# Duo attention with a maxout FFN: masks ahead of the scores, the flags on another queue, and batch 0 rearranged

## The chip, the cores and the metric

The kernel runs on one core of a Trainium2 chip. The metric is the time of one execution in device microseconds (us), as the median of several runs. A profile is taken of one execution; its times count from the start of the span, which is some 2 us shorter than the time of the run. Engines: PE is TensorE's matmuls, PEld its weight loads, DVE is VectorE, ACT is ScalarE, POOL is GpSimd, SP is SyncE. "ACTq", "SPq" and "POOLq" are the queues on which these engines issue transfers.

## The reference

Four batches of eight heads, 768 positions of 64 numbers. Each head is either a "retrieval" head (causal mask) or a "streaming" head (causal, and only the first 4 keys or the last 64 count). Which kind a head is comes as an input, `is_retrieval`, eight integers; below they are called the **flags**. The attention output of all tokens goes through a maxout FFN.

```python
scores = q @ k.T / sqrt(64)
mask   = causal if is_retrieval[h] else causal & (is_sink | in_window)
a      = softmax(where(mask, scores, -1e9))
x      = (a @ v)                      # (4, 8, 768, 64) -> 3072 tokens x 512
h      = maximum(maximum(x @ w1, x @ w2), x @ w3)      # 512 -> 768
out    = h @ w_out                                     # 768 -> 512
```

## The kernel before

The kernel works through 16 score tiles t = 0 to 15: batch, then half of the queries, then four heads. In each it computes transposed scores on PE, exponentiates on ACT, masks on POOL, multiplies by V on PE (with a column of ones that gives the row sums), and divides on DVE. The FFN of a half batch, 18 units of four matmuls and then 3 output blocks, is kept in a queue, and `fill(n)` puts n units of it between the attention work so that PE has something to do while it waits. "FFN (0,0)" below is the FFN of the first half of batch 0, "FFN (0,1)" that of its second half. Instructions are issued to every engine in the order of the program.

The start loads the flags first, on ACT's queue, then K and Q of the four head pairs of batch 0, then V. The weights, the second half of batch 0 and K and Q of the later batches go through POOL's "software" queue, which casts to fp16 where the target is fp16; V of the later batches stays on SP's queue:

```python
nc.scalar.dma_start(out=ir32, in_=is_retrieval ... .to_broadcast([P, 2 * H]))   # the flags
load_pairs(0, 0, 1, (nc.sync, nc.scalar))      # half, first pair, pairs, (queue of K, queue of Q)
load_pairs(0, 1, 1, (nc.sync, nc.scalar))
load_pairs(0, 2, 2, (nc.sync, nc.scalar))
load_v(0, 0)
# ...
def head_flags():                              # first thing that DVE does with data
    nc.vector.tensor_scalar(out=RT, in0=ir32[:, 0 : 2 * H : 2], scalar1=0.0, ..., op0=ALU.not_equal)
    # ... least, far
def head_masks(hp, early=False):               # the two masks of a head pair, from the flags
    # ... nc.vector.tensor_scalar(out=mk[:, h], in0=kept, scalar1=least[:, h : h + 1], ...)
```

K and Q of batch 0 are cast (`cast_pair`), transposed on PE into one PSUM bank, and copied out together (`turn_pair`). For the first two tiles (`NQ` is 2; they are slots 0 to 3) the mask is added in PSUM by an identity matmul that stands after the scores:

```python
def scores(t, u, pairs=(0, 1)):
    early = t < NQ
    # ... the score matmuls:
        nc.tensor.matmul(sts[g // m][...], KQ[rows, 0, ...], KQ[rows, 1, ...],
                         start=(c0 == 0 and r == 0), stop=((b == 0 or r == 1) and not early), ...)
    # ...
        if early:
            # ... nc.tensor.matmul(st[...], ident, mk[...], start=False, stop=True, ...)
        nc.scalar.activation(out=pts[t, i][...], in_=st[...], func=AF.Exp, scale=sc)
```

The order of the start, and the order in the loop over "slots" (one slot is one exp group; slots 4 to 11 belong to batch 0, slot 12 is the first of batch 1):

```python
head_flags()
cast_pair(0, 0, (dve, act))
for hp in range(2):
    head_masks(hp, True)
turn_pair(0, 0, dve)
cast_pair(0, 1, (pool, act))
turn_pair(0, 1, dve)
scores(0, 0, (0,))
cast_pair(0, 2, (dve, pool))
cast_pair(0, 3, (pool, pool))
load_weight(0)                                  # w0t: POOL issues it after its casts
# ... scores, AV, more loads; FFN (0,0) is queued by the last turn_x(1, 1)
fill(2)
for hp in range(2):
    turn_pair(1, hp, dve)
fill(2)
# the loop:
    put(o + (8 if late else 6) + i, late, prep_v, 4 * b + 2, i)      # V casts, on DVE
    put(o + 10 + i, 2, prep_v, 4 * b + 3, i)
    # batch 1's K and Q come in fp16 and are transposed by DVE (eight times 1.14 us):
    put(o + (10 if b == 0 else 8) + 2 * qd + x, 1, turn, b + 1, qd, x, p)
def pace(n):                                    # FFN units per slot
    return 2.4 if n < 14 else 4.0
```

The softmax here doesn't subtract the row's maximum and nothing guards it: scores larger than these inputs give would overflow.

## Time and profile before

| | before |
|---|---|
| time, median of 3 runs | 213.36 us (213.06 to 213.45) |
| span of the profiled run | 211.6 us |
| PE busy | 197.5 us, 93% |
| matmuls | 2132 |

The page's share of the granted TensorE clock in 40 slices (each 5.3 us, in tenths), and its list of what the chain that ended last consists of:

```profile
PEclk9999999999699999999999999999999999999999
PE 74%; DMA 8%; DVE 8%; ACT 4%; issue 2%; POOL 1%; ACTq 0%; DVEq 0%
```

The 6 in the eleventh slice is the spell at half clock that the prediction below speaks of, from 54.3 to 57.7 us in the trace's clock records; it is the only one that this row shows. (The row has no record of the first 6.5 us, where 12 idle matmuls of 512 columns take 5.30 us, twice the 216 ns each that such a matmul takes later.) Lines of the timeline: start, duration, engine and line, what it writes and reads, and in brackets how long the engine had been idle and what ended that.

```profile
0.80 0.42 ACTq L207 DMA_DIRECT2D ir<-in_is_retrieval_dram  x1
...
4.56 0.17 DVE L266 TENSOR_SCALAR RT<-ir 128x8 f32<-128x8 int32 x1 [1.23 <-DMA ir<-in_is_retrieval_dram]
...
...
6.35 0.41 PE L149 MATMUL tr<-ident,kn 128*128 128x128 f16 x3
```

The flags are issued first (0.80), land at 4.54, and DVE makes RT from them at once. K and Q of the first pair land at 5.05 and about 5.8, and PE's first real work, the transposes, starts at 6.35.

### The profile page before, as it was taken

Reading aid. Unit: us, or ns where it says so; the run is one execution under the profiler, and the core shown is the slowest. Engines: PE = TensorE matmul, PEld = TensorE weight load, DVE = VectorE, ACT = ScalarE, POOL = GpSimd, SP = SyncE. Lnnn points to the kernel's source line nnn. Section 1 sums busy time; section 2 is a strip of 40 time slices with the busy share of each in tenths; the row PEclk is TensorE's granted clock in tenths of the full one; section 3 lists DMA queues with packets and bytes.
Section 4 is the critical chain, followed back from the end, with each engine's and each line's share of the span. In section 5 each row is a group of like instructions: output and inputs, shape, how many; then the busy total and the mean of one; then the engine's idle time right before and its main releaser. Section 6 shows DMA issues by size and latency. Waiting matters only on the chain.

```text
span 211.6 us, 5225 instructions
## 1 busy us (share of the span) xinstructions
PE 197.5 (93%) x2132; PEld 112.6 (53%) x2132; DVE 136.5 (65%) x287; ACT 120.5 (57%) x178; POOL 130.0 (61%) x156
## 2 busy tenths in 40 slices
PE   7896889976799999999999999999999999999992
PEld 2454444635456546556566455565565466565550
DVE  3867758689577607996595609996576336554640
ACT  2480896665436686565556675664756766622222
POOL 3399469859994872559995844479944914820000
PEclk9999999999699999999999999999999999999999
DMA  3979999997029568201249397002100120012003
GB/s 103 311 120 277 279 269 213 210 244 219 5 34 164 102 167 230 56 0 54 99 77 156 67 279 173 0 0 102 51 3 0 54 99 3 0 49 103 0 0 150
DMA packets 32396, 23.93 MB, mean 113 GB/s; under 512 B 22837, under 2 KB 27253, under 8 KB 32373
## 3 DMA queue, kind: packets, MB, share of 16 engines
q0 software_dynamic: 4784, 10.23, 24.2%
q1 hardware_dynamic: 26372, 12.59, 20.8%
q10 hardware_dynamic: 1216, 0.79, 1.3%
q8 instruction: 16, 0.26, 0.5%
q14 instruction: 8, 0.06, 0.1%
HBM read 25.17 MB, written 6.29 MB: 149 GB/s over the span
## 4 chain that ended last, share of the span: by engine, by line
PE 74%; DMA 8%; DVE 8%; ACT 4%; issue 2%; POOL 1%; ACTq 0%; DVEq 0%
PE yy L326 37%; PE yy L344 12%; PE st L410 10%; PE oacc L471 8%; DVE KQ L183 4%; PE tr L497 3%; DMA qs<-in_q_dram 3%; ACT pt L432 3%; DMA vs<-in_v_dram 3%; PE yst L326 3%; DMA ks<-in_k_dram 2%; PE yst L344 1%; DVE acc L337 1%; DVE x L481 1%; ACT acc L334 1%
## 5 line engine op out<-in xcount | busy, mean ns | idle before, releaser
L455 POOL TENSOR_TENSOR pt<-pt,mk 128x512 f16<-128x512 f16 x84 | 90.6, 1104 | 35.3 <-ACT pt L432 32.2
L432 ACT ACTIVATE pt<-st 128x1024 f16<-128x1024 f32 (+3 forms) x98 | 83.2, 904 | 23.9 <-PE st L410 20.7
L337 DVE TENSOR_TENSOR acc<-yy,acc 128x384 f16<-128x384 f32 x45 | 25.0, 557 | 39.7 <-ACT acc L334 29.6
L326 PE MATMUL yy<-xT,w0t 128*128 128x384 f16 x180 | 37.1, 331 | 0.3 <-DMA w0t<-in_moe_w_dram 0.3
L334 ACT CAST acc<-yy 128x384 f16<-128x384 f32 x45 | 21.5, 483 | 27.6 <-PE yy L326 23.2
L326 PE MATMUL yy<-xT,w1t 128*128 128x384 f16 x180 | 36.8, 329 | 0.0
L326 PE MATMUL yy<-xT,w2t 128*128 128x384 f16 x180 | 36.3, 326 | 0.0
L410 PE MATMUL st<-KQ 32*128 32x384 f16 (+5 forms) x560 | 29.3, 282 | 5.0 <-DVE rc L479 1.5
L344 PE MATMUL yy<-woutt,hT 128*128 128x512 f16 x132 | 31.6, 379 | 0.0
L337 DVE TENSOR_TENSOR hT<-yy,acc 128x384 f16<-128x384 f32 x45 | 25.0, 557 | 4.3 <-PE yy L326 2.0
L471 PEld LDWEIGHTS <-pt 128*128 128x128 f16 x672 | 24.8, 97 | 5.1 <-issue 1.3
L410 PEld LDWEIGHTS <-KQ 32*128 32x128 f16 (+1 forms) x560 | 12.3, 93 | 24.5 <-issue 15.1
L183 DVE STREAM_TRANSPOSE KQ<-kq 128x384 f32<-128x384 f32 x24 | 24.8, 1138 | 0.0
L471 PE MATMUL oacc<-va,pt 128*128 128x65 f16 x352 | 24.8, 193 | 0.0
L351 ACT COPY ot<-yy 128x512 f32<-128x512 f32 x22 | 13.0, 589 | 20.2 <-PE yy L344 17.4
L326 PEld LDWEIGHTS <-w1t 128*128 128x128 f16 x192 | 17.9, 99 | 12.0 <-issue 2.0
L326 PEld LDWEIGHTS <-w0t 128*128 128x128 f16 x192 | 17.6, 99 | 11.9 <-issue 1.7
L326 PEld LDWEIGHTS <-w2t 128*128 128x128 f16 x192 | 17.6, 98 | 10.4 <-issue 0.4
L471 PE MATMUL oacc<-vf,pt 128*128 128x65 f16 x320 | 21.2, 193 | 0.7 <-DVE hT L337 0.7
L344 PEld LDWEIGHTS <-hT 128*128 128x128 f16 x144 | 13.2, 98 | 14.9 <-issue 1.0
L376 POOL TENSOR_TENSOR vf<-va,far 128x384 f16<-128x384 f16 x16 | 13.2, 826 | 11.8 <-DVE va L374 11.8
L481 DVE TENSOR_TENSOR x<-oacc,rc 128x384 f16<-128x384 f32 x32 | 17.8, 557 | 1.1
(60 smaller groups left out, 139.3 us busy)
## 6 DMA issues: line engine op xcount, KB each, us to landing
out_dram<-ot SPq DMA_DIRECT2D x24, 256.0 KB, 2.2
vs<-in_v_dram SPq DMA_DIRECT2D x21, 256.0 KB, 5.1
kq<-in_k_dram POOLq DMA_DIRECT2D x6, 384.0 KB, 6.3
kq<-in_q_dram POOLq DMA_DIRECT2D x6, 384.0 KB, 7.6
w0t<-in_moe_w_dram POOLq DMA_DIRECT2D x1, 768.0 KB, 8.2
ks<-in_k_dram POOLq DMA_DIRECT2D x2, 384.0 KB, 7.6
qs<-in_q_dram POOLq DMA_DIRECT2D x2, 384.0 KB, 7.8
w1t<-in_moe_w_dram POOLq DMA_DIRECT2D x1, 768.0 KB, 8.7
```

The source lines that it names most:

```text
L183: nc.vector.transpose(out=dst.rearrange("c (p j) -> c j p", j=n)[:, j0:j1], in_=src.rearrange("c (j i) -> c j i", i=R),)
L326: nc.tensor.matmul(yy[:, 0:HALF], w_t[wi][:, ks, ni * P : (ni + 1) * P], xT[b, half][ks], start=(ks == 0), stop=(ks == KS - 1),)
L334: nc.scalar.copy(out=acc[ni], in_=yy[:, 0:HALF])
L337: nc.vector.tensor_tensor(out=dst, in0=yy[:, 0:HALF], in1=acc[ni], op=ALU.max)
L344: nc.tensor.matmul(yo[:, 0:DMdl], hT[ns][:, tb * P : (tb + 1) * P], woutt[:, ns, :], start=(ns == 0), stop=(ns == NNB - 1),)
L351: nc.scalar.copy(out=ot, in_=yo[:, 0:DMdl])
L376: nc.gpsimd.tensor_tensor(out=vf[j][:, hs, k0:k1, 0:D], in0=vs[:, hs, 0:1] if half == 0 else va[j][:, hs, k0:k1, 0:D], in1=far[:, hs, k0:k ...
L410: nc.tensor.matmul(sts[g // m][:, g % m, c0 : c0 + n * P], KQ[rows, 0, ki * P : (ki + 1) * P], KQ[rows, 1, t0 : t0 + n * P], start=(c0 == ...
L432: nc.scalar.activation(out=pts[t, i][:, u, h0 : h0 + m, 0:w], in_=st[:, :, 0:w], func=AF.Exp, scale=sc,)
L455: nc.gpsimd.tensor_tensor(out=x, in0=x, in1=m, op=ALU.mult)
L471: nc.tensor.matmul(o[:, qi, hl, 0 : D + 1], pt[:, u, hl, c : c + P], vv[:, 2 * hp + hl, ki, 0 : D + 1], start=(idx == 0), stop=(idx == len ...
L481: nc.vector.tensor_tensor(out=x, in0=o[:, :, :, 0:D], in1=rc.unsqueeze(3).to_broadcast([P, HB, 2, D]), op=ALU.mult,)
```

## The change

Its intent is to shorten the first 58 us, where PE isn't always busy. (1) The masks enter PSUM first, and the scores are added to them, so that the exp can follow the scores directly. (2) K and Q of the first pair are copied out of PSUM separately. (3) The flags are loaded through GpSimd, so that Q can be issued first on ACT's queue; K and Q of pairs 2 and 3 come in two transfers each. (4) The first tiles' scores, casts and x copies are reordered, some moved to ACT. (5) In the loop of batch 0, V casts go from DVE to ACT, DVE's transposes for batch 1 start earlier, and the FFN units are spread differently.

```diff
-    def load_pairs(half, hp, n, engines):
+    def load_pairs(half, hp, n, engines, alone=False):
+            m = 2 if alone else 2 * n          # (cut: one transfer per pair if alone)
-    def turn_pair(half, hp, op, parts=((0, 1),)):
+    def turn_pair(half, hp, *engines):         # (cut: one bank and one copy per engine given)
-    nc.scalar.dma_start(
+    nc.gpsimd.dma_start(
         out=ir32,
-    load_pairs(0, 2, 2, (nc.sync, nc.scalar))
+    load_pairs(0, 2, 2, (nc.sync, nc.scalar), True)
     # in scores():
+        for x, st in sts.items() if early else ():
+            first = True
+            # (cut) ... ident, mk[...], start=first, stop=False
-                        start=(c0 == 0 and r == 0),
-                        stop=((b == 0 or r == 1) and not early),
+                        start=(c0 == 0 and r == 0 and not early),
+                        stop=(b == 0 or r == 1),
-            if early:
-                # (cut) ... ident, mk[...], start=False, stop=True
     # the start (cut to a part of it):
-    for hp in range(2):
-        head_masks(hp, True)
-    turn_pair(0, 0, dve)
+    head_masks(0, True)
+    turn_pair(0, 0, dve, dve)
-    cast_pair(0, 2, (dve, pool))
+    cast_pair(0, 2, (act, pool))
     for i in range(2):
         prep_v(0, i, pool)
-    load_pairs(1, 0, 2, (nc.gpsimd, nc.gpsimd))
-    # (cut) scores and AV, which move too
     for i in range(2):
         prep_v(1, i, dve)                      # has a multiplication on POOL each
+    load_pairs(1, 0, 2, (nc.gpsimd, nc.gpsimd))
     # (cut)
-    turn_x(0, 0)
-    turn_x(0, 1)
+    turn_x(0, 0, act)
+    turn_x(0, 1, act)
-    fill(2)
+    fill(4)
     # the loop:
-                put(o + i, 2, prep_v, 2 * NQ * b, i)
+                put(o + i, 2, prep_v, 2 * NQ * b, i, act if b == 1 else None)
-            put(o + 10 + i, 2, prep_v, 4 * b + 3, i)
+            put(o + 10 + i, 2, prep_v, 4 * b + 3, i, act if b == 0 else None)
     # (cut: two more lines of the same kind)
-                        put(o + (10 if b == 0 else 8) + 2 * qd + x, 1, turn, b + 1, qd, x, p)
+                        if b == 0:
+                            n, place = 10 + 2 * qd + x, "x" if qd else (0, "x")[p] if x == 0 else 0
+                        else:
+                            n, place = o + 8 + 2 * qd + x, 1
+                        put(n, place, turn, b + 1, qd, x, p)
-        return 2.4 if n < 14 else 4.0
+        return 2.4 if n < 8 else 1.6 if n < 11 else 3.0 if n < 14 else 3.6 if n < 20 else 4.0
```

More of the change, by code (lines that the diff above doesn't have):

```diff
@@ L114 @@
     KQs = {}
-    def load_pairs(half, hp, n, engines):
+    def load_pairs(half, hp, n, engines, alone=False):
         for nm, src, eng in zip(("ks", "qs"), (k, q), engines):
             st = stage.tile([P, 4, HB, D], FP32, tag=nm, name=nm)
-            eng.dma_start(
-                out=st[:, 0 : 2 * n],
-                in_=src[
-                    0, 2 * hp : 2 * hp + 2 * n, half * HALF : (half + 1) * HALF
-                ].rearrange("h (p j) d -> p h j d", p=P),
-            )
+            m = 2 if alone else 2 * n
+            for h in range(0, 2 * n, m):
+                eng.dma_start(
+                    out=st[:, h : h + m],
+                    in_=src[
+                        0, 2 * hp + h : 2 * hp + h + m, half * HALF : (half + 1) * HALF
+                    ].rearrange("h (p j) d -> p h j d", p=P),
+                )
             for i in range(n):
@@ L138, in of_pair @@
         ].rearrange("p (i t) -> p i t", i=2)
-    def turn_pair(half, hp, op, parts=((0, 1),)):
+    def turn_pair(half, hp, *engines):
         if (0, hp // 2) not in KQs:
             KQs[0, hp // 2] = qkt.tile([P, 2, S, 2], FP16, tag="KQ", name="KQ")
-        tr = bank([P, 1024], FP16, "tr")
         xs = cast.pop((half, hp))
-        for part in parts:
-            for i in part:
+        n = 2 // len(engines)
+        for part, op in enumerate(engines):
+            tr = bank([P, 1024], FP16, "tr")
+            for i in range(n):
                 for j in range(HB):
@@ L149, in turn_pair @@
                     nc.tensor.transpose(
-                        tr[:, c : c + P], xs[i][:, j].rearrange("p h d -> p (h d)"), ident
+                        tr[:, c : c + P],
+                        xs[part + i][:, j].rearrange("p h d -> p (h d)"),
+                        ident,
                     )
-            i0, i1 = part[0], part[-1] + 1
             op(
-                out=of_pair(hp)[:, i0:i1, half * HALF : (half + 1) * HALF].rearrange(
-                    "p i (t j) -> p i t j", j=HB
-                ),
-                in_=tr[:, i0 * HALF : i1 * HALF].rearrange(
-                    "p (i j t) -> p i t j", i=i1 - i0, j=HB
-                ),
+                out=of_pair(hp)[
+                    :, part : part + n, half * HALF : (half + 1) * HALF
+                ].rearrange("p i (t j) -> p i t j", j=HB),
+                in_=tr[:, 0 : n * HALF].rearrange("p (i j t) -> p i t j", i=n, j=HB),
             )
@@ L393, in scores @@
                 pts[t, i] = ptp.tile([P, 4, 2, 512], FP16, tag="pt", name="pt")
-        m = 1 if t == 0 and u == 1 else 2
+        m = 1 if u == 1 and (t == 0 or t == 1 and pairs == (0,)) else 2
         if m == 1:
@@ L400, in scores @@
             sts = {i: sps.tile([P, 2, 512], FP32, tag="st", name="st") for i in pairs}
+        for x, st in sts.items() if early else ():
+            first = True
+            for _, u0, _, cols, n, m0 in MASKED[0]:
+                if u0 != u:
+                    continue
+                for hl in range(m):
+                    nc.tensor.matmul(
+                        st[:, hl, cols[0] : cols[0] + n],
+                        ident,
+                        mk[:, 4 * qd + m * x + hl, m0 : m0 + n],
+                        start=first, stop=False, skip_group_check=True,
+                    )
+                first = False
         todo = [(i, part) for i in (pairs if b == 0 else (0,)) for part in UNITS[half][u]]
@@ L420, in scores @@
             i, h0 = m * x // 2, m * x % 2
-            if early:
-                for _, u0, _, cols, n, m0 in MASKED[0]:
-                    if u0 != u:
-                        continue
-                    for hl in range(m):
-                        nc.tensor.matmul(
-                            st[:, hl, cols[0] : cols[0] + n],
-                            ident,
-                            mk[:, 4 * qd + m * x + hl, m0 : m0 + n],
-                            start=False, stop=True, skip_group_check=True,
-                        )
             nc.scalar.activation(
@@ L485, in av, with turn_x @@
         xs[t, i] = x
-    def turn_x(t, i):
+    def turn_x(t, i, op=None):
         b, half, qd = where(t)
@@ L499, in turn_x @@
             )
-        nc.vector.tensor_copy(out=xT[b, half][hp], in_=tr[:, 0:HALF])
+        (op or nc.vector.tensor_copy)(out=xT[b, half][hp], in_=tr[:, 0:HALF])
         if hp == NHP - 1:
@@ L512 @@
     head_flags()
+    head_masks(0, True)
     cast_pair(0, 0, (dve, act))
-    for hp in range(2):
-        head_masks(hp, True)
-    turn_pair(0, 0, dve)
+    head_masks(1, True)
+    turn_pair(0, 0, dve, dve)
     cast_pair(0, 1, (pool, act))
     turn_pair(0, 1, dve)
+    cast_pair(0, 2, (act, pool))
     scores(0, 0, (0,))
-    cast_pair(0, 2, (dve, pool))
+    turn_pair(0, 2, dve)
+    scores(0, 0, (1,))
+    head_masks(2, True)
+    scores(0, 1, (0,))
     cast_pair(0, 3, (pool, pool))
     load_weight(0)
-    head_masks(2, True)
-    scores(0, 0, (1,))
-    turn_pair(0, 2, dve)
-    scores(0, 1, (0,))
     turn_pair(0, 3, dve)
     head_masks(3, True)
+    scores(0, 1, (1,))
     scores(1, 0, (0,))
-    scores(0, 1, (1,))
     scores(1, 0, (1,))
+    scores(1, 1, (0,))
     for i in range(2):
         prep_v(0, i, pool)
-    load_pairs(1, 0, 2, (nc.gpsimd, nc.gpsimd))
-    scores(1, 1, (0,))
-    av(0, 0)
-    av(0, 1)
-    scores(1, 1, (1,))
     for i in range(2):
         prep_v(1, i, dve)
+    load_pairs(1, 0, 2, (nc.gpsimd, nc.gpsimd))
+    av(0, 0)
+    scores(1, 1, (1,))
+    av(0, 1)
     load_weight(1)
     load_pairs(1, 2, 2, (nc.gpsimd, nc.gpsimd))
-    turn_x(0, 0)
-    turn_x(0, 1)
     av(1, 0)
+    turn_x(0, 0, act)
+    turn_x(0, 1, act)
     av(1, 1)
@@ L558 @@
         head_masks(hp)
-    fill(2)
+    fill(1)
     FIRST = 4
@@ L571 @@
             if b > 0:
-                put(o + i, 2, prep_v, 2 * NQ * b, i)
-                put(o + 2 + i, 2, prep_v, 2 * NQ * b + 1, i)
+                put(o + i, 2, prep_v, 2 * NQ * b, i, act if b == 1 else None)
+                put(o + 2 + i, 2, prep_v, 2 * NQ * b + 1, i, act if b == 1 else None)
                 put(o + i, 1, av, 4 * b - 1, i)
@@ L580 @@
             late = 1 if b == 0 else 0
-            put(o + (8 if late else 6) + i, late, prep_v, 4 * b + 2, i)
-            put(o + 10 + i, 2, prep_v, 4 * b + 3, i)
+            put(o + (8 if late else 6) + i, late, prep_v, 4 * b + 2, i, act if b == 0 else None)
+            put(o + 10 + i, 2, prep_v, 4 * b + 3, i, act if b == 0 else None)
             put(o + 8 + late + i, 1, av, 4 * b + 2, i)
```

## The prediction

> **What bounds the kernel now.** I read the page first (busy shares, then the chain that ended last), then the engines' busy times by stretch, then the timeline of the first 60 us, and last the landings of the transfers. The page has PE busy 93% of 211.6 us and 74% of the chain. The stretches show where the other part lies (us; then busy time and count of PE, weight loads, DVE, ACT, POOL; granted clock, DMA share, GB/s):
>
> ```profile
> 8.00:16.00 8.00, 7.44 (x90) 4.40 (x87) 5.97 (x12) 5.97 (x10) 6.37 (x12) 1.00 0.89 172
> 16.00:19.40 3.40, 1.91 (x34) 1.35 (x35) 3.16 (x11) 0.31 (x1) 3.40 (x6) 1.00 1.11 318
> 19.40:43.00 23.60, 22.00 (x217) 12.23 (x217) 15.79 (x34) 17.53 (x25) 17.71 (x20) 1.00 1.12 240
> 43.00:49.00 6.00, 4.06 (x40) 1.72 (x37) 5.81 (x10) 2.68 (x4) 3.59 (x4) 1.00 1.05 253
> 49.00:55.40 6.40, 4.20 (x94) 3.15 (x91) 6.19 (x11) 3.15 (x5) 6.40 (x9) 0.91 0.40 124
> 55.40:58.00 2.60, 2.60 (x16) 1.32 (x14) 0.60 (x2) 2.18 (x3) 2.60 (x4) 0.56 0.01 3
> 130.20:203.90 73.70, 73.66 (x794) 43.39 (x794) 46.02 (x95) 38.75 (x60) 37.74 (x40) 1.00 0.10 37
> ```
>
> From 58 to 204 us PE has work always. Before that it hasn't: from 43 to 55.4 us it is busy 8.3 of 12.4 us while DVE is busy 12.0, and right after it runs at 0.56 of its clock. Busy time hides part of it, so I also took the distance between the starts of neighbouring matmuls, less what each streams (162 ns for 384 columns, 216 for 512, 56 for 128, 32 for an AV matmul, 95 more at a switch between full-height and short tiles). Lost that way: 2.3 us on the half-clock idle matmuls of the start, 5.9 us between 6.5 and 25, 1.3 between 25 and 45, 5.3 between 45 and 58, about 2.5 in all the rest, of which two times 0.5 at 83 and 129 us. A part that touches the first 58 us has some 12 us to win at the very most; PE's own work (about 190 us) is unchanged. The timeline names the waits:
>
> ```profile
> 17.42 0.56 DVE L481 TENSOR_TENSOR x<-oacc,rc 128x384 f16<-128x384 f32 x1
> ...
> 18.03 0.34 PE L497 MATMUL tr<-ident,x 128*128 128x128 f16 x3 [0.58 <-DVE x L481]
> ...
> 19.36 1.47 PE L326 MATMUL yy<-xT,w0t 128*128 128x384 f16 x8 [0.29 <-DMA w0t<-in_moe_w_dram]
> ...
> 21.86 0.34 PE L149 MATMUL tr<-ident,qn 128*128 128x128 f16 x3 [0.58 <-ACT qn L132]
> ...
> 48.42 0.63 PE L410 MATMUL st<-KQ 32*128 32x384 f16 x16 [1.49 <-DVE KQ L183]
> ...
> 54.19 1.00 PE L410 MATMUL st<-KQ 32*128 32x384 f16 x16 [1.51 <-DVE rc L479]
> ```
>
> The last two are the scores of batch 1, which need eight DVE transposes (1.14 us each, from 43.86 to 54.1); the one put down to rc really waits for the transposes just ahead of it, which end at 54.1. No FFN work stands between, as all of FFN (0,0) was issued by 46.5 us. The chain shows the price of the lull:
>
> ```profile
> 55.62 2.39 PE yy L326 x8
> 58.01 0.37 PE oacc L471 x12
> 58.38 1.30 PE yy L326 x8
> ```
>
> Eight FFN matmuls take 2.39 us here and 1.30 anywhere later.
>
> **What the Trainium skill says.** "TensorE: Matmul & The Clock Gate", Part 1, says that an idle window of about 3.4 us drops the array to half clock. The trace agrees in kind: a 3.4 us spell at half clock begins at 54.3 us, though PE was not wholly idle before it. "PSUM — Partial Sum Buffer", The four PSUM rules, says that the first matmul's flag clears a whole bank's marks and later matmuls overwrite unmarked columns and add to marked ones; so the mask may come first and costs what it cost when last. No run shows it yet. "DMA: Bandwidth & Descriptors", Issuing engines are not separate DMA queues, says that another issuer saves sequencer time alone. The trace agrees: the flags' issue took 0.42 us on ACT and Q's first issue came at 1.25 us. "Perfetto Trace Analysis", Optimizing Scalar/DVE Operations, allows moving work to ScalarE where DVE is saturated; here DVE was busy 5.81 of 6.00 us.
>
> **The change part by part.** The order of the built programs gives the same 2132 matmuls; only places and engines move.
>
> *Masks first.* 24 identity matmuls move ahead of the scores. They ran after them in 0.50 us per head pair of 1024 columns. For the first pair I expect nearly nothing: in the new order they stand behind the transposes of pair 1, which end at about 8.0 us because of the Q cast at 7.22, so mask and score still follow each other and the first exp comes at about 8.9 us (8.93 now). The same holds for K and Q evacuated apart (0.96 us becomes two of about 0.5): KQ came at 7.92, pair 1's transposes at 7.95. 0 to 0.3 us.
>
> *Flags by GpSimd, K/Q of pairs 2 and 3 in two transfers each.* Q issues 0.42 us earlier, but landings are spaced by bandwidth (5.05, 6.66, 7.20, 8.37, 9.51 us), so pair 2 may land 0.6 to 1 us earlier and pair 3 as before. POOL's last cast then ends at about 10.0 instead of 11.12 us, where the w0t load is issued. Between 10.6 and 15.9 us the DMA moves only 120 GB/s, from then on some 250 without pause until 45 us: a weight load issued 1 us earlier moves this whole queue (w0t 19.31, ks 20.23, qs 21.21, kq of batch 1 40.29 and 44.33) up to 1 us forward.
>
> *Exp chain and x copies.* ACT's exps of t=0,1 run from 8.93 to 16.31 with 1.0 us idle; without gaps after the second they end at about 15.9. Two of four xT copies (0.35 us) go to ACT and DVE's V casts go ahead of the reciprocals, so DVE's tail from the last exp to the last xT shortens from 3.15 to about 2.8 us. The first FFN matmul starts at about 18.7 instead of 19.36: 0.65 us.
>
> *Four FFN units instead of two before the K/Q transposes.* PE lost 0.27 and 0.74 us there, waiting for ks and qs. Two more units of 0.65 us cover it: 1.2 us. Start to 25 us: 0.65 + 1.2 = about 1.9 us.
>
> *V casts on ACT, transposes earlier, FFN slower.* Eight casts of 0.4 to 0.6 us leave DVE between 36 and 60 us (ACT's Q cast of the same shape took 0.53). The first DVE transpose now stands before slot 10 and no longer behind slot 11's x. Batch 1's first scores (slot 12) have three limits. ACT: from slot 4's exps on, 16 exps (12 of 1.03, 4 of 0.76), one acc copy, 2 Q casts, 2 output copies and 4 V casts of 0.45 sum to 19.9 us, from 23.4 to 24.4: 43.3 to 44.3. DVE: kq's Q half lands at 39.3 to 40.3, then x of 0.75 and two transposes: 43.5 to 44.7. PE: about 42.6. So slot 12 comes at about 44 instead of 48.42, with one FFN unit group of 1.29 us still undone: ahead by 3.1 us. From there: scores 0.65, that group 1.29, AV 0.95, slot 13; slot 14 waits for the last two transposes at about 49.4 to 50, and FFN (0,1) starts at 51 to 52 instead of 55.41. That is 3.4 to 4.4 us, with the gain of the start (1.9) inside. If the lulls, now about 1 us each, no longer trip the half clock, 1.3 us more (eight times 0.16).
>
> After that PE is saturated and the FFN pace only shifts work: 0 (perhaps 0.3 either way at 83 us). Sum: 3.9 (middle) + 0.8 x 1.3 (chance of no half clock) + 0.1 = 5.0 us. 213.36 - 5.0 = **208.3 us**.
>
> **The rivals.** (a) *ACT takes the place of DVE.* It gets eight V casts and two xT copies, and was busy 17.53 of 23.6 us in the main stretch; if exps slip behind casts that wait for V, slots 8 to 12 wait for ACT. For it: 0.7 and 0.5 us of exp-related lulls are already there. Against: ACT is busy 8.0 of the 15 us from 43 to 58. It would leave slot 12 at about 46 and the time at 210 to 210.5. (b) *The DMA sets slot 12 and 14.* If kq lands no earlier, DVE waits at the head of the transposes, its order then holding hT and xT up, and the lull only moves. For it: DMA share above 1.0 from 16 to 45 us. Gain then about 3 us and the half clock may stay: 210.3. (c) *Everything falls in.* Exps start at 8.4, no half clock, the 0.5 us at 83 goes too: 7 us, 206.3. (d) *No gain*, as later work takes it back: PE is full from 58 us on with no wait on another engine, so what is won before must show at the end; unlikely.
>
> **Range and chances.** (a) and (b) together I give 35%, the main line 50%, (c) 15%. Two per cent is 4.2 us, so below about 209.2 counts as faster: main line and (c), with some overlap each way. Time 208.3, range 206.2 to 211.0; faster 0.66, same 0.32, slower 0.02.
>
> **What would show it.** Right: in the chain, the first FFN matmul at 18.4 to 19.0; no wait of PE for the Q cast near 21 us; w0t issued near 10 us; DVE's eight transposes from about 38 to 50 us; the first 16-matmul scores of batch 1 at 43.5 to 45; FFN (0,1) at 51 to 52; eight FFN matmuls there in 1.30, clock 1.00 throughout; the end of the trace after 200 us like before. Wrong: PE's waits of 1 us or more at slots 12 and 14 named ACT or DMA; a half-clock spell after 7 us; w0t landing at 19.3 as before; a first exp at 8.5 or earlier (I undersized the mask part); a new lull after 60 us from the slower FFN pace.

## The result, and the profile after

The changed kernel took 210.86 us (median of 4 runs, 210.43 to 211.60), the kernel before 213.21 us in the runs that go with it. Executions over 1.5% slower than the fastest of the same kernel are left out of the means. Throughout this document a ratio is the mean time of one kernel's runs over that of the other's runs of the same rounds, so it isn't quite the ratio of the medians quoted. Here it is 0.9895, with a 95% interval of 0.9861 to 0.9929: a gain of 2.35 us by the medians, where 5.0 had been forecast. All outputs were correct, here and in every experiment below.

The page's clock row and chain of the changed kernel:

```profile
PEclk9979999999999999999999999999999999999998
PE 80%; DVE 10%; DMA 3%; ACT 2%; issue 1%; POOL 1%; POOLq 0%; ACTq 0%
PE yy L328 38%; PE yy L346 13%; PE st L425 10%; PE oacc L475 9%; DVE KQ L185 5%; PE tr L501 3%; DMA ir<-in_is_retrieval_dram 3%; PE yst L328 3%; DVE x L485 2%; ACT pt L436 2%; PE tr L152 2%; PE st L409 1%; PE yst L346 1%; DVE KQ L157 1%; DVE rc L483 1%
```

The half-clock slice at 55 us is gone, as hoped. A new one stands third from the left: the clock records have half clock from 9.9 to 13.3 us, right after PE stood idle from 6.56 to 9.81. And a name has come into the chain that wasn't listed before: the transfer of the flags, with 3% of the span, for 8 KB. The timeline of the start:

```profile
1.32 0.72 POOL L209 DMA_DIRECT2D ir<-in_is_retrieval_dram  x1 [0.81 <-POOLq L649]
...
8.11 0.17 DVE L268 TENSOR_SCALAR RT<-ir 128x8 f32<-128x8 int32 x1 [3.54 <-DMA ir<-in_is_retrieval_dram]
...
9.81 0.46 PE L152 MATMUL tr<-ident,kn 128*128 128x128 f16 x3 [3.25 <-POOL kn L134]
```

Q is issued 0.44 us earlier, as predicted, and the first K and Q land at 4.02 and 4.25 instead of 5.05 and about 5.8. But the flags, issued at 1.32, land at 8.09: 6.8 us from issue to landing, where ACT's queue had needed 3.7. RT is DVE's first instruction that needs data. DVE works in order, so its cast of K waits behind it (and behind the first pair's masks, which the change put ahead of the cast) although K is there, and the first transposes start at 9.81 instead of 6.35. (The bracket names POOL's cast, which ended at nearly the same moment; the weight load ahead of it waited for DVE's kn.)

That isn't all. One stretch of the kernel before (us; busy time and count of PE, weight loads, DVE, ACT, POOL; granted clock, DMA share, GB/s):

```profile
5.00:6.00 1.00, 1.00 (x4) 0.38 (x3) 0.95 (x5) 0.17 (x1) 0.47 (x2) 1.00 1.01 330
```

And three of the changed one:

```profile
4.00:5.00 1.00, 1.00 (x3) 0.29 (x2) 0.34 (x3) 0.78 (x3) 0.00 (x0) 1.00 1.06 213
5.00:6.00 1.00, 1.00 (x4) 0.29 (x2) 0.00 (x0) 0.00 (x0) 0.00 (x0) 1.00 0.95 64
6.00:7.00 1.00, 0.56 (x2) 0.00 (x0) 0.00 (x0) 0.00 (x0) 0.00 (x0) 1.00 0.65 143
```

The last number of a line is the rate at which data moved. It falls to 64 GB/s, where the kernel before had 330, while the DMA engines are still "busy" 95% of the time. In the queues' view of the first 12 us of the changed kernel one sees with what (packets, MB, share of 16 engines):

```profile
q1 hardware_dynamic: 4023, 1.53, 49.7%
...
q0 software_dynamic: 32, 0.01, 9.4%
```

32 packets with a hundredth of a megabyte took 9.4% of the engines' time, 18 us in all (0.094 x 12 x 16), where the 1.53 MB on SP's queue, K and V, took 49.7%. The 16 that carry data (512 bytes each) took 0.38 to 1.77 us, 1.1 on average. So the transfer of the flags through GpSimd was late itself, and while it ran little else moved. The second Q landed at 8.27 instead of 7.20, and all four pairs were there at 10.26 instead of 9.51.

The middle of the batch went much as forecast. The stretches that the prediction shows, now:

```profile
8.00:16.00 8.00, 5.89 (x51) 3.92 (x52) 6.92 (x17) 3.70 (x7) 6.19 (x14) 0.79 0.97 192
...
43.00:49.00 6.00, 5.80 (x69) 2.97 (x68) 5.97 (x11) 4.45 (x9) 4.75 (x6) 1.00 0.93 218
49.00:55.40 6.40, 4.89 (x99) 3.41 (x98) 4.70 (x9) 4.78 (x8) 6.40 (x8) 1.00 1.06 272
55.40:58.00 2.60, 2.60 (x27) 1.60 (x25) 1.10 (x4) 1.63 (x3) 2.60 (x4) 1.00 0.67 149
```

From 43 to 55.4 us PE is busy 10.7 us instead of 8.3, and the clock is 1.00 from 49 to 58 us. From 8 to 16 us, on the other hand, PE is busy 5.89 us instead of 7.44, at a clock of 0.79. The points along the way, in us:

| | before | after |
|---|---|---|
| first transpose of K | 6.35 | 9.81 |
| first FFN matmul, FFN (0,0) | 19.36 | 22.05 |
| first scores of batch 1, slot 12 | 48.42 | 47.84 |
| first matmul of FFN (0,1) | 55.41 | 55.04 |

The changed kernel is 2.7 us behind at its first FFN matmul and 0.6 ahead at slot 12. By the measure of the prediction (the distance between the starts of neighbouring matmuls, less what each streams) PE loses 9.75 us before 25 us where it lost 8.3, 1.8 from 25 to 45 where it lost 1.3, and 2.2 from 45 to 60 where it lost 5.3. With the rest of the span that is 15.8 instead of 17.6 us, and the difference, 1.8, fits that of the two spans (211.6 - 209.9 = 1.7). So from 25 us on 2.6 us were won, of the 3.1 that the prediction's sum gives to the loop and the clock, and the start, meant to win 1.9, lost about 1.5.

### The profile page after: what moved, and what is told of

It is laid out like the page before. It is cut to its first block, busy times and chain, and to the rows that moved or that the text cites. A ratio compares the mean times of both kernels' runs of the same rounds, so it can differ in the third digit from the quotient of the medians.

```text
span 209.9 us, 5236 instructions
## 1 busy us (share of the span) xinstructions
PE 196.0 (93%) x2132; PEld 112.7 (54%) x2132; DVE 132.1 (63%) x277; ACT 125.1 (60%) x190; POOL 129.4 (62%) x157
## 3 DMA queue, kind: packets, MB, share of 16 engines
HBM read 25.17 MB, written 6.29 MB: 150 GB/s over the span
## 4 chain that ended last, share of the span: by engine, by line
PE 80%; DVE 10%; DMA 3%; ACT 2%; issue 1%; POOL 1%; POOLq 0%; ACTq 0%
PE yy L328 38%; PE yy L346 13%; PE st L425 10%; PE oacc L475 9%; DVE KQ L185 5%; PE tr L501 3%; DMA ir<-in_is_retrieval_dram 3%; PE yst L328 3%; DVE x L485 2%; ACT pt L436 2%; PE tr L152 2%; PE st L409 1%; PE yst L346 1%; DVE KQ L157 1%; DVE rc L483 1%
## 5 line engine op out<-in xcount | busy, mean ns | idle before, releaser
L328 PE MATMUL yy<-xT,w1t 128*128 128x384 f16 x180 | 36.3, 326 | 0.9 <-DVE acc L339 0.9
L328 PE MATMUL yy<-xT,w0t 128*128 128x384 f16 x180 | 36.3, 326 | 0.0
L483 DVE RECIPROCAL rc<-oacc 128x6 f32<-128x6 f32 x32 | 6.1, 191 | 29.8 <-PE oacc L475 29.5
L328 PEld LDWEIGHTS <-w1t 128*128 128x128 f16 x192 | 17.6, 98 | 12.9 <-issue 3.0
L328 PEld LDWEIGHTS <-w2t 128*128 128x128 f16 x192 | 17.6, 98 | 10.6 <-issue 0.5
```

The source lines that it names most:

```text
L328: nc.tensor.matmul(yy[:, 0:HALF], w_t[wi][:, ks, ni * P : (ni + 1) * P], xT[b, half][ks], start=(ks == 0), stop=(ks == KS - 1),)
L483: nc.vector.reciprocal(out=rc, in_=o[:, :, :, D])
```

## The experiments

The theory after this reading: the loop part is worth what was forecast or more, the start part would be worth something, and the flags' transfer takes 2 to 3 us away, by holding the DMA engines or by DVE's waiting for it. The rivals: the start's reordering itself is at fault (ACT has too much to do there); or the loop part was worth less than forecast.

### flags_back and flags_back2: the changed kernel, with the flags again first on ACT's queue

```diff
-    nc.gpsimd.dma_start(
+    nc.scalar.dma_start(
         out=ir32,
```

> The changed kernel with one edit: the flags are loaded from ScalarE's queue again, ahead of Q, as before. Theory (late flags): the flags landed at 8.09 us from GpSimd against 4.54 before, VectorE stood in order behind them, and PE's first transpose came at 9.81 instead of 6.35 us; so the first transpose returns to 6.2 to 6.5 us, the flags land at 4.5 to 5, and the time falls by about 3 us to 207.0 to 208.3. Rival (hidden): the loads and the transposes of batch 1 set the pace up to 50 us anyway, so the start moves but the time stays within 1 us of the changed kernel: 210 to 211.

Measured: 208.79 us (the five fast runs, 208.25 to 209.01; just above the 207.0 to 208.3 expected), ratio to the kernel before 0.9776 (0.9737 to 0.9814). Its profiled execution, however, took 487.11 us, more than twice as long as any of the other five, and counts as slow. The same program was run again on another chip:

> The same program as flags_back, whose profiled run had all matmuls at a third of their rate (487 us) and can't be read: a profile in the fast state, and the time again: 208.2 to 209.2. If the start is really about 3 us earlier than in the changed kernel, the first transpose stands at 6.2 to 6.5 us and w0t lands at 16 to 17.5; where the time then goes is open: theory (loads set batch 1): kq lands no earlier than 40 us and slot 12 no earlier than 46, as in the start part alone; rival (ScalarE's chain of exps sets slot 12): slot 12 starts right at the end of ScalarE's work on slot 11.

Measured: 208.78 us (208.54 to 209.18), ratio 0.9806 (0.9779 to 0.9834). This one line of the change thus costs 210.86 - 208.78 = 2.1 us (these ran on different occasions; the difference of the two ratios gives 1.9). The start of its trace, from the stretches and the timeline:

```profile
5.00:6.00 1.00, 0.96 (x4) 0.25 (x2) 0.95 (x6) 0.81 (x1) 0.56 (x2) 1.00 1.06 344
```

```profile
6.48 0.34 PE L152 MATMUL tr<-ident,kn 128*128 128x128 f16 x3 [0.52 <-DVE kn L134]
...
9.66 0.93 POOL L297 DMA_DIRECT2D w0t<-in_moe_w_dram  x1
...
18.11 2.88 PE L328 MATMUL yy<-xT,w0t 128*128 128x384 f16 x16
```

The rate is back at 344 GB/s, the transposes start at 6.48, the first FFN matmul at 18.11 instead of 22.05. So the start's rearrangement isn't at fault for the lateness of 22.05, and that rival falls. Of what was expected here, K of batch 1 landed a little earlier than the 40 us (39.49), and slot 12 came at 44.99, not after 46.

### flags_alone: the kernel before, with nothing changed but the flags

```diff
-    nc.scalar.dma_start(
+    nc.gpsimd.dma_start(
         out=ir32,
```

> The kernel before with one edit: the flags are loaded by GpSimd. Theory (late flags): about 3 us slower than before, 215.5 to 217, with the flags landing at 7.5 to 8.5 us and packets of over 1 us on the flags' queue. Rival (hidden): within 0.7 us of before, 213 to 214, since its PE waited for loads and batch 1 in any case.

Measured: 218.30 us (216.65 to 219.31) against 213.38, ratio 1.0218 (1.0166 to 1.0270). The flags landed at 8.61, the first transpose started at 9.74 and the first FFN matmul at 24.05. So this part, taken alone, makes the kernel slower by 4.9 us, more than twice what it costs in the changed kernel, and more than the 215.5 to 217 expected. The effects of the parts don't add. The first FFN matmul comes 4.7 us later than before here, and 3.9 later than with the flags back there. The clocks of the runs may explain a part of the rest: the time follows the mean clock, from 216.65 and 216.90 us at 0.981 and 0.984 to 219.09, 219.19 and 219.31 at 0.966. A mean of 0.966 means that some 15 us ran at half clock (2 x 0.034 x 217), where the changed kernel's profile has 3.4 us in the middle of its span. How much of the 4.9 us is the clock alone no run here separates.

### flags_spare: the flags early, and a second copy through GpSimd that nobody reads

Does DVE's wait for the flags cost the time, or does the transfer slow the others? Here the kernel of flags_back gets a second load of the same 8 KB, through GpSimd, into a tile that nothing uses.

```diff
+    spare = consts.tile([P, 2 * H], mybir.dt.int32, name="spare")
+    nc.gpsimd.dma_start(out=spare, in_=is_retrieval ... .to_broadcast([P, 2 * H]))
     load_pairs(0, 0, 1, (nc.sync, nc.scalar))
```

> flags_back with a second copy of the flags that GpSimd loads at the same place and nobody reads. Theory A (the software transfer itself holds the DMA engines: in both kernels that have it [...]all engines' rate fell from about 330 to 60 kB per us between 4 and 6.5 us): K and Q land late again (second Q after 8 us), first transpose may still be early, and the time is 1 to 2 us above flags_back2. Theory B (only the wait on the late flags costs): time as flags_back2 within 0.5 us.

Measured: 210.63 us (210.19 to 211.57), ratio 0.9900 (0.9872 to 0.9927), against 208.78 without the copy, on the same chip in the same rounds. The copy that no instruction waits for costs 1.85 us, of the 2.1 that the flags' move costs. From its stretches, its queues in the first 12 us, and its timeline:

```profile
5.00:6.00 1.00, 1.00 (x4) 0.30 (x2) 0.92 (x6) 0.56 (x1) 0.38 (x2) 1.00 0.99 115
```

```profile
q0 software_dynamic: 32, 0.01, 7.3%
...
spare<-in_is_retrieval_dram POOLq DMA_DIRECT2D x1, 8.0 KB, 6.1
```

```profile
6.66 0.46 PE L152 MATMUL tr<-ident,kn 128*128 128x128 f16 x3
...
9.24 0.34 PE L152 MATMUL tr<-ident,qn 128*128 128x128 f16 x3 [1.34 <-ACT qn L134]
...
9.91 0.51 POOL L134 CAST qn<-qs 128x384 f16<-128x384 f32 x1 [3.25 <-DMA qs<-in_q_dram]
```

The flags' own transfer lands at 4.94 and RT isn't late any more (4.96), and the first transposes run at 6.66. Yet the rate drops to 115 GB/s at 5 to 6 us, Q of the later pairs comes late, PE and POOL stand waiting for it, and the load of w0t, which POOL issues after its casts, goes out at 11.27 instead of 9.66. The first FFN matmul starts at 21.07, against 18.11 without the copy and 22.05 in the changed kernel. So the slow transfer by itself suffices for nearly the whole cost, and DVE's wait adds little to it (0.2 us). What DVE's wait would cost without the slow transfer no run shows.

One more rival has to go: half clock. A spell of it begins at 9.9 to 10.4 us in the profiles of all three kernels that load the flags or the copy through GpSimd (3.4 us long, 6.8 in flags_alone), and flags_back2 has none. Is the spell what the copy costs? The runs settle it. A spell of 3.4 us takes 0.008 off the mean clock (half of 3.4 in 209 us). Three runs of flags_spare have a mean of 0.996 to 1.000, so no such spell, and took 210.19, 210.58 and 211.34 us; the three with 0.990 to 0.992 took 210.45, 210.68 and 211.57. The copy costs its time without the spell too.

Why its packets are so slow no record here tells. That the first packets of POOL's queue are slow in other kernels too is seen in the kernel before: the first 30 packets of w0t, the first thing on that queue there, took 433 ns on average (960 at most), most later ones of their size 135.

### loop_part: the kernel before, with the loop's part of the change alone

```diff
     # before, plus:
+                put(o + i, 2, prep_v, 2 * NQ * b, i, act if b == 1 else None)   # and three like it
+                        if b == 0:
+                            n, place = 10 + 2 * qd + x, "x" if qd else (0, "x")[p] if x == 0 else 0
+        return 2.4 if n < 8 else 1.6 if n < 11 else 3.0 if n < 14 else 3.6 if n < 20 else 4.0
```

> The kernel before with the loop part alone (V casts of the loop on ScalarE, transposes of batch 1 earlier, FFN pace). Prediction's sum: 2.0 us in the middle and 1.3 us from the half clock that is not tripped: 209.9 to 211. Rival: the loop part brings only the 1.3 us of the clock, as the lull stays where the kq loads land: 212.

Measured: 209.25 us (209.09 to 210.04) against 213.38, ratio 0.9810 (0.9775 to 0.9846): 4.1 us, more than the 209.9 to 211 expected. The rival that the loop was worth less than forecast falls. Two stretches, and two lines of the timeline:

```profile
43.00:49.00 6.00, 5.66 (x69) 3.03 (x67) 5.95 (x10) 4.67 (x7) 4.58 (x6) 1.00 1.00 223
49.00:55.40 6.40, 6.26 (x94) 3.94 (x96) 4.05 (x9) 4.96 (x10) 6.40 (x9) 1.00 1.01 278
```

```profile
46.31 0.64 PE L410 MATMUL st<-KQ 32*128 32x384 f16 x16
...
50.88 1.11 PE L410 MATMUL st<-KQ 32*128 32x384 f16 x16
```

The two groups of scores that PE used to wait for, 1.49 us at 48.42 and 1.51 us at 54.19, now start at 46.31 and 50.88 with no wait in brackets. PE is busy 11.9 of 12.4 us (before: 8.3), at full clock.

### loop_no_vcast, loop_no_turns and loop_no_pace: which piece of the loop does it

Each takes one of the three pieces out of loop_part again. The first edit (with three lines like it), then the second, then the third:

```diff
-                put(o + i, 2, prep_v, 2 * NQ * b, i, act if b == 1 else None)
+                put(o + i, 2, prep_v, 2 * NQ * b, i)
```

```diff
-                        if b == 0:
-                            n, place = 10 + 2 * qd + x, "x" if qd else (0, "x")[p] if x == 0 else 0
-                        else:
-                            n, place = o + 8 + 2 * qd + x, 1
-                        put(n, place, turn, b + 1, qd, x, p)
+                        put(o + (10 if b == 0 else 8) + 2 * qd + x, 1, turn, b + 1, qd, x, p)
```

```diff
-        return 2.4 if n < 8 else 1.6 if n < 11 else 3.0 if n < 14 else 3.6 if n < 20 else 4.0
+        return 2.4 if n < 14 else 4.0
```

> The loop part on the kernel before without its V casts: transposes of batch 1 and FFN pace moved, V casts still on VectorE. Theory (VectorE is the limit from 43 to 55 us, and each cast of 0.4 to 0.6 us there delays a transpose): 1 to 2 us slower than the loop part, 210.3 to 211.3. Rival (FFN work left for the lull does it all): within 0.5 us of the loop part, 208.8 to 209.8.

> The loop part on the kernel before without the earlier place of batch 1's transposes (V casts and FFN pace stay). Theory: the transposes start behind slot 11's x again, at about 43.5 us instead of 40.0, so slot 12 comes 1.5 to 2.5 us later and 1.5 to 2.5 us are lost: 210.8 to 211.8. Rival (without the V casts VectorE has room, the place is of no matter): within 0.6 us of the loop part, 208.7 to 209.9.

> The loop part on the kernel before without the FFN pace. Theory (VectorE): the transposes come early, so at most 1 us is lost: 209.3 to 210.3. Rival (FFN left for the lull): the lull stays empty, PE drops to half clock again and 2 us or more are lost: 211.3 to 212.5.

Measured:

| kernel | us | range | ratio to before | loss against 209.25 |
|---|---|---|---|---|
| loop_no_vcast | 211.74 | 211.34 to 212.13 | 0.9945 (0.9921 to 0.9968) | 2.5 |
| loop_no_turns | 210.98 | 210.26 to 213.30 | 0.9910 (0.9864 to 0.9955) | 1.7 |
| loop_no_pace | 209.81 | 209.45 to 209.95 | 0.9848 (0.9820 to 0.9875) | 0.6 |

These three ran on other chips than loop_part, each beside the kernel before, which was the same there within 0.3 us (213.08 and 213.16 against 213.38). The three losses sum to 4.8 us, not less than the 4.1 of all together, so nothing suggests that two of the pieces win the same time; the 0.6 of the pace is not clear of the noise. Expected were losses of 1 to 2, 1.5 to 2.5 and at most 1 us, so the V casts were worth more than thought. The rival that without the pace the half clock comes back at 55 us falls: the clock is 1.00 from 49 to 58 us. The profile of loop_no_turns fell on its slowest run (213.30, with Q late at the start), so only its times are used. For the V casts the view of the tile `va` shows what ACT does better. In loop_part, from 36 to 62 us (duration in ns as least/median/most):

```profile
L374 ACT CAST va<-vs x8: 512/514/522, 36.2 to 58.8; 128x384 f16<-128x384 f32 x8
```

In loop_no_vcast:

```profile
L374 DVE CAST va<-vs x8: 349/724/2670, 36.6 to 61.0; 128x384 f16<-128x384 f32 x8
```

DVE took anything from 0.35 to 2.67 us for the cast that takes ACT 0.51. The Trainium skill has a reason: "SBUF — State Buffer", SBUF: two separate sides, says that VectorE (in its faster modes) and GpSimd lock a pair of ports against each other for a whole instruction, and that ScalarE has ports of its own. The trace agrees as far as it goes: the four longest casts (0.91, 1.25, 1.02 and 2.67 us) all met mask multiplications of POOL, and each ended 0.21 to 0.23 us after the end of one. No run here tests it alone. With the casts on DVE the two groups of scores start at 47.40 and 53.49, and the second waits again. (A part of that delay may be a half-clock spell from 19.0 to 22.4 us, which this profile has and that of loop_part has not. The loss stands without it: three runs with a mean clock of 0.996 to 1.000 took 211.34 to 211.63 us.)

```profile
53.49 0.63 PE L410 MATMUL st<-KQ 32*128 32x384 f16 x16 [0.98 <-DVE KQ L183]
```

### start_part: the changed kernel, flags back, the loop's part undone

```diff
     # flags_back, and in the loop the three edits above
```

> The changed kernel with the flags on ScalarE's queue and the loop as before (V casts of the loop on VectorE, transposes of batch 1 where they were, FFN pace as before): the start part alone. Prediction's sum: 1.9 us from the start, so about 211.3. Rival: the start gains nothing alone because batch 1's first scores wait for VectorE, and the lull at 46 to 54 us only grows: 213 to 213.5.

Measured: 213.96 us (212.57 to 215.47) against 213.38, ratio 1.0021 (0.9967 to 1.0076): no gain, as the rival said and not as the prediction's sum had it. Yet the first FFN matmul starts at 17.58, 1.8 us earlier than before. Its timeline shows where that goes:

```profile
25.20 0.82 PE L328 MATMUL yy<-xT,w1t 128*128 128x384 f16 x4 [0.38 <-DMA w1t<-in_moe_w_dram]
...
47.58 0.64 PE L425 MATMUL st<-KQ 32*128 32x384 f16 x16 [2.00 <-DVE KQ L185]
```

And the stretch after it:

```profile
49.00:55.40 6.40, 5.12 (x71) 3.46 (x68) 5.38 (x11) 2.52 (x5) 6.40 (x8) 0.50 0.67 169
```

w0t is issued at 9.43 (before: 11.12) and lands at 16.41 (19.31), as the prediction hoped. But POOL issues the next loads only at 14.21 and 15.02, after its work on V (before: 13.89 and 14.71). POOL first waits 1.18 us for V to land, and the change itself had moved these loads behind two more of POOL's multiplications on V (`prep_v(1, ...)`), which no part of the prediction counted. So nothing of the gain is passed on: w1t lands at 25.15 (24.89), woutt at 38.35 (36.54), K of batch 1 at 40.18 (38.39). PE, being early, waits for w1t at 25.20. Slot 12 still waits for DVE, 2.00 us now, so it is only 0.8 us earlier than before; FFN (0,1) starts at 54.98 (55.41). And the half clock holds from 48.9 to about 59.1 us (by the trace's clock records; the stretch above lies within it), where before it held from 54.3 to 57.7. FFN (0,1) runs at half pace for 4.1 us instead of 2.3 (59.1 - 54.98 and 57.7 - 55.41), which costs an estimated 0.9 us more: 0.4 gained, 0.9 lost, and the medians differ by 0.6. The other runs bear it out: the two whose mean clock is like that of the kernel before (0.989 and 0.991) took 212.78 and 212.57 us, the four with 0.968 to 0.980 took 213.94 to 215.47.

In the company of the loop part the start is worth 209.25 - 208.79 = 0.5 us (loop_part and flags_back, same chip and rounds).

### masks_last: flags_back with the masks after the scores again, and K and Q of the first pair together

```diff
-    turn_pair(0, 0, dve, dve)
+    turn_pair(0, 0, dve)
     # and in scores() the identity matmuls after the scores, as in the kernel before
```

> flags_back with the masks added after the scores again and K and Q of pair 0 evacuated together. The prediction gave these two parts 0 to 0.3 us: 208.7 to 209.2, with the first exp 0 to 0.3 us later than in flags_back2. Rival (the intent of the change: masks off the path of the first scores): the first exp 0.5 us or more later and the time 0.5 to 1 us longer, 209.3 to 209.8.

Measured: 208.82 us (208.54 to 209.67), ratio 0.9804 (0.9773 to 0.9836), against 208.78. The first exp starts at 9.21 instead of 8.80 (0.4 us, between the two expectations; the profiled run was the slowest of the six, 209.67), and in the median nothing of that reaches the end. The part that gives the change its name is worth nothing measurable here.

### loads_early: flags_back, with the next loads issued right behind the first weight

start_part suggests that the loads' order on POOL's queue holds the gain of the start back. Here K and Q of the second half (pairs 0 and 1) are issued right after w0t and no longer after the V work. This kernel is meant to beat both.

```diff
     cast_pair(0, 3, (pool, pool))
     load_weight(0)
+    load_pairs(1, 0, 2, (nc.gpsimd, nc.gpsimd))
     ...
     for i in range(2):
         prep_v(1, i, dve)
-    load_pairs(1, 0, 2, (nc.gpsimd, nc.gpsimd))
```

> flags_back with one more edit: the second half of K and Q of pairs 0 and 1 is issued by GpSimd right after w0t and no longer behind the V work of the start. Theory (the chain of software loads binds): in flags_back2 that queue ran dry from w0t's landing at 16.75 us to ks at 19.50, and PE lost 1.05 us at 20.7 waiting for them; now ks and qs land 1 to 2 us earlier, the lull at 20.7 goes, kq of batch 1 lands about 1 us earlier, and the time falls 0.8 to 2 us below flags_back2: 206.8 to 208.0. Rival (VectorE and ScalarE in the middle bind, not the loads): within 0.4 us of flags_back2, 208.4 to 209.2.

Measured: 207.93 us (207.63 to 208.39) against 213.16, ratio 0.9758 (0.9725 to 0.9791). It is the fastest of all: 5.2 us faster than the kernel before, 2.9 faster than the changed one by the medians. The two loads go out at 10.40 and 11.16 (flags_back2: 14.39 and 15.20), w1t lands at 23.54 (25.17), K of batch 1 at 37.04 (39.49). The chain of waits of flags_back2 passes through the load of batch 1's K on its way to slot 12 (start, us, what):

```profile
25.46 14.04 DMA kq<-in_k_dram
...
44.99 0.84 PE st L425 x14
```

That of loads_early, of which one line is shown, has no load of batch 1 in it before slot 12:

```profile
44.28 0.92 PE st L425 x14
```

Slot 12 comes 0.7 us earlier, and the end 0.85. That is within the expectation, though its path was another in part: ks and qs landed only 0.6 us earlier, not 1 to 2.

## Why the prediction was right or wrong, point by point

- **The bound, and where the gain lies: right.** PE was the bound from 58 us on, and what was won before showed at the end, as in loop_part, loads_early and flags_back2.
- **V casts on ACT, earlier transposes, FFN pace: right in kind, sized too low.** Forecast were 3.4 to 4.4 us at FFN (0,1) with 1.9 of the start inside, so about 2.0 for the loop, and 1.3 for the half clock: 3.3. The loop alone measured 4.1, of which about 3.5 without any half clock (next point), where 2.0 were forecast. Slot 12 came at 46.31 (loop_part) and 44.99 (flags_back2), not at 44 as worked out; FFN (0,1) at 52.10 in both, against 51 to 52. One of the prediction's three limits for slot 12 was summed wrongly: 39.3 to 40.3 plus 0.75 and two transposes of 1.14 is 42.3 to 43.3, not 43.5 to 44.7; the limit by ACT (43.3 to 44.3) gave the 44 in any case.
- **The half clock: right, but sized too high.** In the profiles the clock is 1.00 from 49 to 58 us wherever the loop part is in, and eight FFN matmuls of FFN (0,1) take 1.42 us in the chain of the changed kernel, not 2.39. But the prediction took one profile for every run. Of the 33 runs of the kernel before in the experiments, 15 have a mean clock of 0.996 or more, which leaves no room for a 3.4 us spell, and took 212.66 us on average; the other 18 (0.992 or less) took 213.71. The spell thus costs about 1.05 us and not 1.3 (the prediction's own chain lines give 2.39 - 1.30 = 1.09), and only about half of the runs have it. On the chip of loop_part the runs without a spell took 212.71 us before and 209.19 in loop_part: 3.5 us, won without the clock.
- **Masks first, K and Q apart, "0 to 0.3 us": right.** masks_last measured 0.0 (the ratios' intervals leave some 0.6 us either way).
- **Flags by GpSimd: the step that failed.** The prediction put it so: "Q issues 0.42 us earlier, but landings are spaced by bandwidth", and then "a weight load issued 1 us earlier moves this whole queue". It counted what leaves ACT's queue and took the transfer of 8 KB on the other queue as free. It asked neither when the flags would land nor what they would do to the others. They landed 3.6 us later (8.09 against 4.54), the rate of all transfers fell to 64 GB/s, w0t was issued at 11.29 (before: 11.12; forecast: near 10). The term should have been about -2.1 us (flags_back2); the transfer alone gives 1.85 of it (flags_spare). None of the rivals named this. Rival (b) saw the DMA as a risk, but later in the kernel. Of the prediction's own signs of being wrong, one came: a half-clock spell after 7 us (9.9 to 13.3).
- **Start to 25 us, "about 1.9 us": mis-sized.** With the flags back, the first FFN matmul came at 18.11, 1.25 us earlier than before and 0.6 better than the 18.7 forecast. But the step that "a weight load issued 1 us earlier moves this whole queue" failed here as well: the loads behind w0t stood behind POOL's V work, and w1t landed at 25.17 in flags_back2, later than before (24.89). Nor did four FFN units cover the wait ahead of the K/Q transposes: PE still waits 0.88 us at 21.88 (before: 0.58 at 21.86). Net worth beside the loop part: 0.5 us. In kind this is rival (b), and moving two loads (loads_early) gave 0.85 us of it back.
- **The sum.** Forecast 5.0 = 1.9 (start) + 3.1 (loop and clock: 2.0 + 0.8 x 1.3 + 0.1). Measured 4.1 (loop) + 0.5 (start) - 2.1 (flags) = 2.5, against 2.35 (5.0 forecast); as each term is the step from one kernel to the next, this sum must come out and is no further proof. With the flags on their old queue the kernel takes 208.78 us, close to the 208.3 forecast, but that is luck in part: the start was 1.4 us short and the loop 1.0 us over.
- **Rival (a), ACT in DVE's place:** not seen. In the chain of the changed kernel ACT has 2% where it had 4. PE waits 0.65 us in loop_part for the V that follows ACT's cast, but 0.56 and 0.53 also where DVE casts (loop_no_vcast).
- **Open:** why software packets of 512 bytes take 1.1 us on average; how much of the 4.9 us that the flags cost in the kernel before, against 2.1 in the changed one, is half clock; what DVE's wait for late flags costs without the slow transfer; what the 487 us run was.

## What to carry to other kernels

A tiny transfer isn't free because it is tiny: before moving it to another queue, look in the trace at how long that queue's transfers take to land, who stands behind its first reader in program order, and what the data rate does while it runs. A start that becomes earlier is worth only what the loads behind it let through, so the issue of those loads has to move with it. Read the mean clock of every run, not only that of the profiled one: here nearly half of the runs of the kernel before had no half-clock spell. To judge a bundle of edits, run each part alone and the whole without it: here one line gave back nearly half of what the rest had won (2.1 of 4.6 us).

## What the Trainium skill lacked or had wrong

- "DMA: Bandwidth & Descriptors", Anatomy of one DMA, fits a transfer issued from GpSimd with about 2.0 us plus the bytes at 436 GB/s, which is an estimated 2.02 us for 8 KB. The same 8 KB took 6.8 us from issue to landing in the changed kernel, 7.3 in flags_alone and 6.1 as the copy in flags_spare, each time beside the loads of K and Q. On ScalarE's queue, beside the same loads, they took 3.7 to 4.1.
- The same page, Issuing engines are not separate DMA queues, says that another issuer only saves the sequencer's time, which by itself leads one to expect no harm. In flags_spare one 8 KB transfer through GpSimd, which nobody read, took the rate of all transfers from 344 to 115 GB/s (5 to 6 us) and cost 1.85 us. That a small software transfer can hold up all others is missing.
- "SBUF — State Buffer", SBUF: two separate sides, offers one cause for slow GpSimd transfers: VectorE keeps GpSimd from writing descriptors, and the DMA engines sit idle. For the slowness of the packets under way it isn't this one: in the changed kernel VectorE was busy 0.00 us from 5 to 7 us, and the DMA engines had a share of 0.95 from 5 to 6. (Whether it has to do with their first start, at 4.36 us, no run shows.)
- "TensorE: Matmul & The Clock Gate", Part 1, ties half clock in its table to an idle window of about 3.4 us, and only for one other kernel tells of short idles that do it. In start_part half clock began at 48.9 us, and the longest wait of PE in the ten us before was 2.0; in flags_spare it began at 10.4 us, and the longest wait from 7 us on was 1.34. So PE needn't be idle all that time. How idle it must be the page doesn't say.
